# The start of an attention and MLP kernel on one core: summary rows through GpSimd's queue, another order of the first transfers, the third quad's scores ahead of the sums of values

## The chip, the cores and the metric

The kernel runs on one core of a Trainium2 chip. The metric is the device time of one launch in microseconds (us). Before the change the median of three runs is 639.26 us (638.43 to 639.28).

## The reference

Attention over 768 positions in 4 batches and 8 heads of 64 numbers. Each query sees the keys less than 16 positions away and, beside them, 24 summaries of blocks of 32 positions: the maximum of the block's keys and the mean of its values. The result, 3072 tokens of 512 numbers, goes through an MLP.

```
k_sum = k.reshape(B, H, nb, 32, D).max(axis=3)
v_sum = v.reshape(B, H, nb, 32, D).mean(axis=3)
scores_l = where(|i - j| < 16, q @ k.T / 8, -1e9)
scores_s = q @ k_sum.T / 8 + log(32)
a = softmax(concatenate([scores_l, scores_s]))
x = a @ concatenate([v, v_sum])          # -> [3072, 512]
h = x @ w_in                             # [3072, 2048]
out = (h * erf(softplus(h))) @ w_out     # [3072, 512]
```

The inputs q and k are drawn eight times larger than v, and all is f32.

## The kernel before

**Tiles.** The tokens are cut into 6 chunks of 512 tokens. A chunk's attention is done in 4 *quads*, one for each pair of heads (24 quads, numbered from 0; quads 0 to 3 belong to the first chunk and are called the first to the fourth below). A chunk's hidden layer is done in 4 *hidden blocks* of 512 hidden numbers, each in four quarters of 128; the stretch of the kernel for one hidden block is a *period* (24 periods). Products of the MLP take each f32 operand as a high and a low part in a shorter format and add three matmuls (L625, L690); only the output products of the first two periods use f32 as it is (L686).

**One quad.** TensorE makes scores (L501) into one bank or two, for the first quads with the mask added by matmuls (L485, L486). VectorE takes row maxima (L525, later L521), negates and scales them (L540), ScalarE makes eight exponentials with their row sums (L531), VectorE adds 1e-9, inverts (L535, L543) and scales by the sums (L547). TensorE turns the probabilities (L561), ScalarE copies them (L565), TensorE multiplies them by the values (L586), and the result x is split into high and low (L268 and L602).

**One period.** Four hidden products (L625, each of 12 matmuls, one quarter of a hidden block) go into banks h0 and h1 in turn (the first four into h0, h1, o0, o1). From each, ScalarE takes a tanh (L636) and VectorE or ScalarE a copy of h (L268). Then ScalarE takes logarithms (L649) and error functions (L654), VectorE multiplies (L661 in the first two periods, L666 later) and splits (L268, L673), and TensorE adds the output product (L690, L686). ScalarE's tanh, logarithm and erf are in different tables, and a change of table is an instruction of its own (L891).

**Summaries.** For the first batch K's block maxima come from the natural layout of K (tiles `kf`, L424, VectorE). The sums of V come from TensorE: `vsum_first` multiplies six tiles of V by a matrix `pick` (L430, six matmuls into a bank named `vs`), ScalarE copies the result (L433), and rows of it are laid into the tile of values of each of the first four quads: for the first quad by a copy on GpSimd (L436), for the other three by a DMA that SP issues (L438). For later batches K and V are loaded in natural layout into a shared tile `rows` (L372, L373), VectorE reduces them (L380, L381), TensorE turns V's sums (L388), ScalarE copies them (L390). GpSimd lays K's maxima into later quads' K tiles (L456, 28 copies).

**Transfers.** All loads go through SP's queue in one order: K and Q of the first four quads (L413, L414), V for the sums (`vt`, L418), V rows of the first four quads (`vwf`, L421), 16 units of weights (`rw`, L301, 1 MB each; VectorE puts their numbers together in three steps, then ScalarE casts the high part, L268, and VectorE takes the low part), then later quads' K, Q and V (L451, L447, L465, L469). A load that has to wait for a tile to come free, or for data to send, holds up what stands behind it in the queue.

**What sets the order.** Every step is recorded in a `Plan` with the engines that can do it and a cost for each. `Plan.due` gives each step a due time by TensorE's order, and `Plan.order` plays the engines against each other and picks, whenever an engine is free, the step with the lowest key: its number (TensorE) or due time (the others), plus an offset from the table `TUNE` (step number: offset, price of a change of table, choice of table, engine). The instructions are then issued in the order found. TensorE may pull a step forward only near the start (a window of 60 steps for steps under 330). In the last loop, until a bank named o3 is first written, `busy` (L728) puts filler matmuls on zeros where the plan has TensorE waiting over 0.3 us; 18 of them stand ahead of everything.

```
busy(math.ceil((gap + (0.8 if free_at < 16.0 else 0.2)) / 0.11) if gap > 0.3 else 0)
```

Of the kernel before, what the change touches and what calls it, by code (L numbers as in the profile page):

```python
# [26 lines left out]
NB = T // 64  # L27
NI = NB // 2
NT = T // 128
NS = 24  # L30
LW = 96
NK = LW + NS
# [8 lines left out]
NN = 2  # L41
TABLE = 1.29
PEN = 1.5
TUNE = {138: (-4.0, 1.5, 0, None), 161: (13.0, 1.5, 0, None), 168: (0.0, 3.0, 0, None), 198: (0.0, 1.5, 0, 'DVE'), 207: (13.0, 1.5, 0, None), 212: (13.0, 1.5, 0, None), 240: (-9.0, 1.5, 0, None), 241: (-5.0, 1.5, 0, None), 371: (22.0, 1.5, 0, None), 498: (0.0, 1.5, 0, 'ACT'), 511: (3.0, 1.5, 0, None)}
LAT = {"PE": 0.25, "DVE": 0.2, "ACT": 0.24, "POOL": 0.3, "SP": 2.0}


# [130 lines left out]
def block_attention_mlp(ctx: ExitStack, tc: tile.TileContext, q_t, k_nat, k_win, v_tok, v_nat, v_win, w_in, w_out, out):  # L178
    nc = tc.nc
# [7 lines left out]
    def sb(shape, dtype, name, tag=None):  # L187

        n = math.prod(shape[1:])
        if n % 128 == 0:  # L190
            return pool.tile(shape, dtype, name=name, tag=tag or name)
        t = pool.tile([128, -(-n // 128) * 128], dtype, name=name, tag=tag or name)[0:shape[0], 0:n]
        return t if len(shape) == 2 else t.rearrange("p (a b) -> p a b", a=shape[1]) if len(shape) == 3 else t.rearrange("p (a b c) -> p a b c", a=shape[1], b=shape[2])

    def ps(name, tag):
        return psum.tile([128, 2, 512] if tag == "pa" else [128, 512], F32, name=name, tag=tag)
# [50 lines left out]
    vsum = sb([NK, NP, 128], F32, "vsum")  # L247
# [7 lines left out]
    def pe(us, fn, r=(), w=(), **kw):  # L255
        return P.add({"PE": us}, lambda e: fn(), r, w, **kw)

    def on(us, fn, r=(), w=(), **kw):
        return P.add(us, lambda e: fn(engines[e]), r, w, **kw)

    def act(us, fn, r=(), w=(), **kw):
        return P.add({"ACT": us}, lambda e: fn(), r, w, **kw)

    def dma(kb, fn, r=(), w=(), hold=2.0, **kw):
        return P.add({"SP": max(0.45, kb / 350.0)}, lambda e: fn(), r, w, hold=hold, **kw)
# [135 lines left out]
    st = {}  # L401
# [24 lines left out]
    def vsum_first(bank):  # L426
        def go(t):
            if t == 0:
                tiles[bank] = ps("vs", bank)
            nc.tensor.matmul(tiles[bank][0:NK], lhsT=pick[:, 20 - 4 * t:140 - 4 * t], rhs=vts[t // 3][:, t % 3], start=(t == 0), stop=(t == 5))  # L430
        for t in range(6):
            pe(0.87, lambda t=t: go(t), [f"vt{t // 3}"], [bank])
        act(0.5, lambda: nc.scalar.copy(vsum[LW:NK], tiles[bank][LW:NK].rearrange("s (p c) -> s p c", p=NP)), [bank], [f"vsum0{p}" for p in range(NP)])  # L433
        for p in range(NP):
            if p == 0:
                on({"POOL": 1.1}, lambda e: e.tensor_copy(st[0]["vw"][LW:NK], vsum[LW:NK, 0:1, :].to_broadcast([NS, NB, 128])), ["vsum00"], ["vwg0"])  # L436
            else:
                dma(100, lambda p=p: nc.sync.dma_start(out=st[p]["vw"][LW:NK], in_=vsum[LW:NK, p:p + 1, :].to_broadcast([NS, NB, 128])), [f"vsum0{p}"], [f"vwg{p}"])  # L438


    def load_quad(qd):
# [283 lines left out]
    def busy(n):  # L725

        for _ in range(n):
            nc.tensor.matmul(idle[:, 0:256], lhsT=zeros[:, 0:128], rhs=zeros, start=True, stop=True)  # L728
# [10 lines left out]
    for p in range(3):  # L739
        ksum_first(p)  # L740
        scores(p, banks[p])
        softmax(p, banks[p])
    vsum_first("o2")
    ksum_first(3)
    scores(3, banks[3])
# [133 lines left out]
    free = {"PE": 5.0, "DVE": 1.4, "ACT": 4.2, "POOL": 5.2, "SP": 0.7}  # L879
    plan = P.order(free, lambda n: 60 if n < 330 else 0, TUNE, "exp")  # L880
    sets = {"exp": "exp_and_others", "log": "natural_log_exp_and_others", "sig": "sigmoid_and_others"}
    free_at, filling = free["PE"], True
    for o in plan:
        if o["on"] == "PE":
            filling = filling and "o3" not in o["w"]
            if filling:
                gap = o["start"] - free_at
                busy(math.ceil((gap + (0.8 if free_at < 16.0 else 0.2)) / 0.11) if gap > 0.3 else 0)
            free_at = o["end"]
        if "load" in o:  # L890
            nc.scalar.preload_act_table_set(sets[o["load"]])  # L891
        o["fn"](o["on"])
# [40 lines left out]
```

## Time and profile before

| what | before |
|---|---|
| median of three runs | 639.26 us |
| the profiled execution | 639.46 us |
| its span on the core | 637.6 us |
| TensorE busy | 631.5 us (99%) |
| VectorE busy | 393.8 us (62%) |
| ScalarE busy | 432.7 us (68%) |
| GpSimd busy | 18.6 us (3%) |
| granted clock of TensorE | 1.00 |

The lines quoted below come from one profiled execution. In the views of groups and of the timeline a line gives start and length in us, the engine, the source line and operation, the tile written and the tiles read, the count, and in brackets the idle time ahead of it with what ended it. PE is TensorE's matmuls, PEld its weight loads, DVE VectorE, ACT ScalarE, POOL GpSimd, SP the engine that issues transfers. The chain of waits is followed back from the last instruction; its lines give start, length, engine, tile and line.

### The profile page before, as it was taken

To read this page: it belongs to the slowest core of one execution; us is meant where nothing else is said; L and a number is where in the kernel's file an instruction comes from. 1 tells how busy PE (TensorE), PEld (TensorE's weight loads), DVE (VectorE), ACT (ScalarE), POOL (GpSimd) and SP (SyncE) were. 2 spreads that over 40 slices of the span, in tenths; PEclk is the share of its full clock that TensorE was granted. 3 is DMA by queue.
4 is the path that set the end of the run, shared out by engine and by line. 5 is a ranking of instruction groups with operands and counts; after the bars stand their busy time and mean duration, and the time that the engine had idled before them with its cause. 6 is when DMAs were issued, how large, how long until landed. Compare 5 with 4: busy or idle time off the path is not lost.

```text
span 637.6 us, 10591 instructions
## 1 busy us (share of the span) xinstructions
PE 631.5 (99%) x4288; PEld 505.8 (79%) x4288; DVE 393.8 (62%) x507; ACT 432.7 (68%) x779; POOL 18.6 (3%) x56
## 2 busy tenths in 40 slices
PE   9999999999999999999999999999999999999997
PEld 6786566888888888878888888888888888888886
DVE  4999999873975574576655745745555454334432
ACT  5749999969868567676494785675865852863460
POOL 2100011000000000000000000000000000000000
PEclk9999999999999999999999999999999999999999
DMA  8999775753454062752242640223451103140013
GB/s 325 271 343 348 254 227 178 251 180 110 174 161 129 1 213 96 225 182 64 66 149 90 205 149 1 79 73 139 145 177 33 32 1 133 66 133 1 1 62 136
DMA packets 28485, 89.33 MB, mean 140 GB/s; under 512 B 3028, under 2 KB 8468, under 8 KB 23316
## 3 DMA queue, kind: packets, MB, share of 16 engines
q1 hardware_dynamic: 27860, 88.13, 41.9%
q8 instruction: 34, 0.56, 0.4%
q10 hardware_dynamic: 576, 0.52, 0.2%
q14 instruction: 15, 0.12, 0.1%
HBM read 75.89 MB, written 10.49 MB: 135 GB/s over the span
## 4 chain that ended last, share of the span: by engine, by line
PE 91%; ACT 4%; DVE 2%; DMA 2%; issue 0%; SPq 0%; DVEq 0%
PE ops L690 38%; PE h L625 36%; PE px L586 4%; PE pa L501 3%; PE pa L561 3%; PE ops L686 2%; PE idle L728 2%; ACT L891 1%; DMA out<-rows 1%; PE vs L430 1%; DMA rows<-k_nat 1%; ACT wt L649 1%; PE h L501 0%; ACT wt L636 0%; ACT pr L531 0%; DVE hc L268 0%
## 5 line engine op out<-in xcount | busy, mean ns | idle before, releaser
L625 PE MATMUL h<-xh,w 128*128 128x512 f32 x768 | 250.0, 395 | 0.3 <-ACT vsum L390 0.3
L690 PE MATMUL ops<-w,gh 128*128 128x512 f32 x704 | 223.2, 392 | 0.0
L625 PEld LDWEIGHTS h<-xh,w 128*128 128x128 f32 x768 | 144.1, 188 | 32.0 <-issue 1.4
L636 ACT ACTIVATE wt<-h 128x512 f32<-128x512 f32 x96 | 57.3, 598 | 154.1 <-DVE hc L268 84.3
L690 PEld LDWEIGHTS ops<-w,gh 128*128 128x128 f32 x704 | 132.6, 188 | 27.8
L625 PE MATMUL h<-xl,w 128*128 128x512 f32 x384 | 149.4, 389 | 0.0
L891 ACT ACT_TABLE_LOAD x106 | 136.0, 1283 | 1.8
L690 PE MATMUL ops<-w,gl 128*128 128x512 f32 x352 | 137.2, 390 | 0.0
L268 DVE COPY hc<-h 128x512 f32<-128x512 f32 x88 | 60.7, 690 | 123.1 <-PE h L625 115.1
L625 PEld LDWEIGHTS h<-xl,w 128*128 128x128 f32 x384 | 72.2, 188 | 15.2 <-issue 1.0
L690 PEld LDWEIGHTS ops<-w,gl 128*128 128x128 f32 x352 | 66.1, 188 | 13.2
L666 DVE TENSOR_TENSOR hc<-wt,hc 128x1024 f32<-128x1024 f32 x44 | 52.5, 1222 | 19.0 <-ACT wt L654 19.0
L649 ACT ACTIVATE wt<-wt,stats 128x1024 f32<-128x1024 f32 x48 | 55.3, 1153 | 0.6
L531 ACT ACTIVATE pr<-pr,stats 128x120 f32<-128x120 f32 x128 | 48.8, 382 | 9.0 <-DVE stats L540 8.9
L673 DVE TENSOR_TENSOR gl<-hc,gh 128x1024 fp32r<-128x1024 f32 x44 | 52.4, 1220 | 0.2
L654 ACT ACTIVATE wt<-wt 128x1024 f32<-128x1024 f32 x48 | 49.2, 1054 | 0.3
L268 DVE CAST gh<-hc 128x1024 fp32r<-128x1024 f32 x44 | 30.1, 690 | 24.8 <-PE ops L690 24.1
L535 DVE TENSOR_SCALAR stats<-stats 128x8 f32<-128x8 f32 x24 | 4.2, 175 | 43.1 <-ACT pr L531 41.5
L686 PE MATMUL ops<-a32s,gw 128*128 128x512 f32 x64 | 29.0, 594 | 0.0
L565 ACT COPY ptr<-pa 120x1024 f32<-120x1024 f32 x24 | 24.1, 1004 | 3.3 <-PE pa L561 3.3
L456 POOL COPY kw<-ksum 128x96 f32<-128x96 f32 (+1 forms) x28 | 13.1, 480 | 443.5 <-DMA kw<-k_win 383.8
L586 PEld LDWEIGHTS px<-ptr,vw 120*64 120x64 f32 x640 | 20.3, 138 | 5.4 <-issue 3.1
(109 smaller groups left out, 523.1 us busy)
## 6 DMA issues: line engine op xcount, KB each, us to landing
w<-dr SPq DMA_DIRECT2D x20, 1024.0 KB
kw<-k_win SPq DMA_DIRECT2D x20, 480.0 KB
rw<-w_in SPq DMA_DIRECT2D x8, 1024.0 KB
rw<-w_out SPq DMA_DIRECT2D x8, 1024.0 KB
vw<-v_win SPq DMA_DIRECT2D x20, 384.0 KB
qb<-q_t SPq DMA_DIRECT2D x20, 256.0 KB
rows<-v_nat SPq DMA_DIRECT2D x12, 384.0 KB
rows<-k_nat SPq DMA_DIRECT2D x12, 384.0 KB
```

The costliest lines, as they stand in the source:

```text
L268: e.copy(o, i) if e is nc.scalar else e.tensor_copy(o, i)
L531: nc.scalar.activation(s["pr"][:, j], s["pr"][:, j] if qd >= MQ else s["sc"][j // NI][:, i * NK:(i + 1) * NK], AF.Exp, scale=0.125, bias=s ...
L586: nc.tensor.matmul(xo[r, o], lhsT=s["vw"][:, j, r], rhs=s["pt"][:, a, o], start=True, stop=True)
L625: nc.tensor.matmul(hs[k, f][:, 0:T], lhsT=w[m], rhs=xt[ch, cc][x], start=(cc == 0 and n == 0), stop=(cc == 3 and n == 2))
L636: nc.scalar.activation(wt[k, f // 2][:, f % 2], hs[k, f][:, 0:T], AF.Tanh, scale=0.5)
L649: act(1.06, lambda n=n: nc.scalar.activation(wt[k, n], wt[k, n], AF.Ln, scale=-0.49999994, bias=half_b), [s], [s], table=("log",))
L654: act(0.96, lambda n=n: nc.scalar.activation(wt[k, n], wt[k, n], AF.Erf, scale=-1.0), [s], [s], table=("sig",), after=after)
L666: e.tensor_tensor(hc[k, n], wt.pop((k, n)), hc[k, n], op=ALU.mult)
L673: e.tensor_tensor(gs[k, n][1], hc.pop((k, n)), f32(gs[k, n][0]), op=ALU.subtract)
L686: nc.tensor.matmul(os_[ch, t], lhsT=x[0][:, i % 2, t * 128:(t + 1) * 128], rhs=w32["o", g, i // 2][:, i % 2], start=first, stop=last)
L690: nc.tensor.matmul(os_[ch, t], lhsT=x[y][:, i % 2, t * 128:(t + 1) * 128], rhs=w[m], start=first and n == 0, stop=last and n == 2)
L891: nc.scalar.preload_act_table_set(sets[o["load"]])
```

## The change

Three pieces of code change.

1. Rows of V's summaries for the second to fourth quad (L438) are sent by GpSimd's queue instead of SP's.
2. The rule for fillers is the same wherever they stand: the gap plus 0.3 us (it was plus 0.8 before 16 us of the plan and plus 0.2 after).
3. `TUNE` has 117 entries instead of 11. They move steps up to number 797 of the plan, and by that transfers, steps of VectorE and ScalarE and, up to about 260 us, of TensorE; behind that TensorE's order is the same.

```diff
-TUNE = {138: (-4.0, 1.5, 0, None), 161: (13.0, 1.5, 0, None),
...
+TUNE = {0: (-450.0, 1.5, 0, None), 1: (-443.0, 1.5, 0, None), 2: (-339.0, 1.5, 0, None), 3: (-556.0, 1.5, 0, None),
...
             if p == 0:
                 on({"POOL": 1.1}, lambda e: e.tensor_copy(st[0]["vw"][LW:NK], vsum[LW:NK, 0:1, :].to_broadcast([NS, NB, 128])), ["vsum00"], ["vwg0"])
             else:
-                dma(100, lambda p=p: nc.sync.dma_start(out=st[p]["vw"][LW:NK], in_=vsum[LW:NK, p:p + 1, :].to_broadcast([NS, NB, 128])), [f"vsum0{p}"], [f"vwg{p}"])
+                on({"POOL": 2.5}, lambda e, p=p: e.dma_start(out=st[p]["vw"][LW:NK], in_=vsum[LW:NK, p:p + 1, :].to_broadcast([NS, NB, 128])), [f"vsum0{p}"], [f"vwg{p}"])
...
             if filling:
                 gap = o["start"] - free_at
-                busy(math.ceil((gap + (0.8 if free_at < 16.0 else 0.2)) / 0.11) if gap > 0.3 else 0)
+                busy(math.ceil((gap + 0.3) / 0.11) if gap > 0.3 else 0)
```

The entries of `TUNE` say little by themselves, so here is what they do at three places. First the order on TensorE where the third quad's scores (into the banks o0 and o1, here `o_281` and `o_282`) meet the sums of values (`vs`). Before:

```order
L728 MATMUL idle<-zeros 128x256
L430 MATMUL vs<-vt,pick 120x512 x2
L485 LDWEIGHTS small
L485 MATMUL o_281<-mask_h,small 128x480
...
L430 MATMUL vs<-vt,pick 120x512 x4
L561 MATMUL pa<-ident,prf 120x128 x8
L728 LDWEIGHTS zeros
```

Two of the six sums stood ahead of the third quad's scores, behind fillers. The same place on TensorE after the change (the scores' banks are now `o_262` and `o_263`; the first row is the last of the second quad's scores):

```order
L501 MATMUL h_211<-ksum,qf 64x24
L485 LDWEIGHTS small
L485 MATMUL o_262<-mask_h,small 128x480
...
L501 MATMUL o_263<-ksum,qf 64x24
L430 MATMUL vs<-vt,pick 120x512 x6
L561 MATMUL pa<-ident,prf 120x128 x8
L485 LDWEIGHTS small
```

The third quad's scores now follow the second quad's directly, and all six sums come behind them.

The second place is SP's queue of transfers, from the first unit of weights on. Before:

```order
L301 DMA rw<-w_in 128x2048
L414 DMA qf<-q_t 128x512
L421 DMA vwf<-v_win 96x1024 x2
L301 DMA rw<-w_in 128x2048
L438 DMA vwf<-vsum 24x8x128
L421 DMA vwf<-v_win 96x1024
L438 DMA vwf<-vsum 24x8x128
L301 DMA rw<-w_in 128x2048
L421 DMA vwf<-v_win 96x1024
L301 DMA rw<-w_in 128x2048
L438 DMA vwf<-vsum 24x8x128
L373 DMA rows<-v_nat 128x768
```

The three transfers of summary rows stood between V rows and weights. SP's queue after the change:

```order
L301 DMA rw<-w_in 128x2048
L414 DMA qf<-q_t 128x512
L421 DMA vwf<-v_win 96x1024
L301 DMA rw<-w_in 128x2048
L421 DMA vwf<-v_win 96x1024 x2
L301 DMA rw<-w_in 128x2048 x2
L421 DMA vwf<-v_win 96x1024
L373 DMA rows<-v_nat 128x768
L301 DMA rw<-w_out 128x2048
L372 DMA rows<-k_nat 128x768
L451 DMA kw<-k_win 128x960
L373 DMA rows<-v_nat 128x768
```

The summary rows have left it. A second load of `rows<-v_nat` has moved ahead of later weights. They stand on GpSimd now, behind its copy for the first quad:

```order
L251 MEMSET pick 32x1 x4
L436 COPY vwf<-vsum 24x1024
L438 DMA vwf<-vsum 24x8x128 x3
L456 COPY kw<-ksum 128x4x24 x8
L456 COPY kw<-ksum 128x8x24 x8
```

Ahead of the place shown, SP's first transfers are reordered too: before they ran K, Q, K, Q, K, `vt`, Q, `vt`, K, and now Q, K, Q, Q, K, K, K, `vt`, `vt`.

The third place is VectorE near 273 us of the profile of before, where it takes the maxima of a later batch's K (L380). Before:

```order
L268 COPY hc<-h 128x512 x3
L380 TENSOR_REDUCE ksum<-rows 128x24
L268 COPY hc<-h 128x512
L515 TENSOR_TENSOR pr<-pa,mask_sb 128x960
L268 CAST xh<-px 128x512
L521 TENSOR_REDUCE stats<-pr 128x8
```

The maxima stood between the third and the fourth copy of a period. On VectorE after the change, from the last two of these copies on:

```order
L268 COPY hc<-h 128x512 x2
L515 TENSOR_TENSOR pr<-pa,mask_sb 128x960
L268 CAST xh<-px 128x512
L521 TENSOR_REDUCE stats<-pr 128x8
L602 TENSOR_TENSOR xl<-px,xh 128x512
L540 TENSOR_SCALAR stats<-stats 128x8
L381 TENSOR_REDUCE vs_sum<-rows 128x24
L380 TENSOR_REDUCE ksum<-rows 128x24
```

The maxima now come behind the softmax's row maxima and behind the sums of V.

On ScalarE the order of the first periods' functions changes as well: it loads tables 13 times instead of 16 up to the last erf of the third hidden block, and 108 times instead of 106 in all. The scaling by the sums of the fourth quad moves from VectorE to ScalarE (as eight instructions), one cast of x moves from ScalarE to VectorE, and two copies of h in this stretch move from VectorE to ScalarE.

More of the change, by code (lines that the diff above doesn't have):

```diff
@@ L43 @@
 PEN = 1.5
-TUNE = {138: (-4.0, 1.5, 0, None), 161: (13.0, 1.5, 0, None), 168: (0.0, 3.0, 0, None), 198: (0.0, 1.5, 0, 'DVE'), 207: (13.0, 1.5, 0, None), 212: (13.0, 1.5, 0, None), 240: (-9.0, 1.5, 0, None), 241: (-5.0, 1.5, 0, None), 371: (22.0, 1.5, 0, None), 498: (0.0, 1.5, 0, 'ACT'), 511: (3.0, 1.5, 0, None)}
+TUNE = {0: (-450.0, 1.5, 0, None), 1: (-443.0, 1.5, 0, None), 2: (-339.0, 1.5, 0, None), 3: (-556.0, 1.5, 0, None), 4: (-259.0, 1.5, 0, None), 5: (-402.0, 1.5, 0, None), 6: (-246.0, 1.5, 0, None), 7: (-93.0, 1.5, 0, None), 8: (-221.0, 1.5, 0, None), 9: (-144.0, 1.5, 0, None), 10: (-86.0, 1.5, 0, None), 13: (50.0, 1.5, 0, None), 14: (-105.0, 1.5, 0, None), 15: (-87.0, 1.5, 0, None), 68: (-196.0, 1.5, 0, None), 70: (-296.0, 1.5, 0, None), 75: (301.0, 1.5, 0, None), 79: (118.0, 1.5, 0, 'DVE'), 91: (-176.0, 1.5, 0, None), 94: (-157.0, 1.5, 0, None), 107: (92.0, 1.5, 0, None), 108: (39.0, 1.5, 0, None), 109: (39.0, 1.5, 0, None), 110: (175.0, 1.5, 0, None), 115: (103.0, 1.5, 0, None), 124: (92.0, 1.5, 0, None), 127: (168.0, 1.5, 0, None), 128: (139.0, 1.5, 0, None), 130: (546.0, 1.5, 0, None), 131: (177.0, 1.5, 0, None), 132: (332.0, 1.5, 0, None), 138: (333.0, 1.5, 0, None), 140: (65.0, 1.5, 0, 'DVE'), 152: (-172.0, 1.5, 0, None), 154: (485.0, 1.5, 0, None), 155: (511.0, 1.5, 0, None), 157: (147.0, 1.5, 0, None), 169: (265.0, 1.5, 0, 'DVE'), 176: (-138.0, 1.5, 0, None), 178: (-89.0, 1.5, 0, None), 180: (171.0, 1.5, 0, None), 181: (123.0, 1.5, 0, None), 184: (233.0, 1.5, 0, None), 191: (4.0, 8.0, 1, None), 195: (43.0, 1.5, 0, None), 201: (347.0, 1.5, 0, None), 202: (-53.0, 2.0, 0, None), 206: (228.0, 1.5, 0, None), 209: (133.0, 1.5, 0, None), 210: (765.0, 1.5, 0, None), 211: (348.0, 1.5, 0, None), 227: (387.0, 1.5, 0, None), 230: (194.0, 1.5, 0, None), 240: (-501.0, 1.5, 0, None), 243: (279.0, 1.5, 0, None), 244: (426.0, 1.5, 0, None), 247: (-372.0, 1.5, 0, None), 253: (289.0, 1.5, 0, None), 255: (177.0, 1.5, 0, None), 267: (-182.0, 1.5, 0, 'ACT'), 275: (-378.0, 1.5, 0, None), 276: (142.0, 1.5, 0, None), 279: (-120.0, 1.5, 0, None), 281: (285.0, 1.5, 0, None), 303: (314.0, 1.5, 0, None), 305: (-218.0, 1.5, 0, 'ACT'), 311: (-231.0, 1.5, 0, 'ACT'), 316: (231.0, 1.5, 0, None), 320: (96.0, 3.0, 1, None), 325: (172.0, 1.5, 0, None), 327: (-158.0, 1.5, 0, None), 335: (223.0, 1.5, 0, None), 336: (311.0, 1.5, 0, None), 338: (-72.0, 1.5, 0, None), 341: (185.0, 1.5, 0, None), 342: (266.0, 1.5, 0, None), 343: (913.0, 1.5, 0, None), 345: (469.0, 1.5, 0, None), 346: (435.0, 1.5, 0, None), 366: (-404.0, 1.5, 0, None), 383: (-204.0, 1.5, 0, 'ACT'), 446: (231.0, 1.5, 0, None), 472: (-514.0, 1.5, 0, None), 480: (315.0, 1.5, 0, None), 481: (189.0, 2.0, 1, None), 489: (-218.0, 1.5, 0, None), 509: (171.0, 1.5, 0, None), 519: (-96.0, 1.5, 0, None), 529: (112.0, 1.5, 0, None), 531: (98.0, 1.5, 0, None), 545: (169.0, 1.5, 0, None), 552: (90.0, 1.5, 0, None), 553: (251.0, 1.5, 0, None), 567: (132.0, 1.5, 0, None), 591: (176.0, 1.5, 0, None), 593: (194.0, 1.5, 0, None), 594: (232.0, 1.5, 0, None), 599: (236.0, 1.5, 0, None), 603: (444.0, 1.5, 0, None), 621: (319.0, 1.5, 0, None), 624: (291.0, 1.5, 0, None), 638: (198.0, 1.5, 0, None), 675: (190.0, 1.5, 0, None), 680: (189.0, 1.5, 0, None), 682: (215.0, 1.5, 0, None), 692: (-123.0, 1.5, 0, None), 700: (184.0, 1.5, 0, None), 705: (-398.0, 1.5, 0, None), 717: (163.0, 1.5, 0, None), 721: (-149.0, 1.5, 0, None), 722: (244.0, 1.5, 0, None), 732: (103.0, 1.5, 0, None), 733: (34.0, 1.5, 0, None), 740: (123.0, 1.5, 0, None), 754: (259.0, 1.5, 0, None), 789: (-79.0, 7.0, 0, None), 797: (-110.0, 1.5, 0, None)}
```

## The prediction

> **What bounds the kernel now.** I read the page first, then the chain that ended last, TensorE's timeline and waits, the stages, and then the start engine by engine.
>
> ```profile
> span 637.6 us, 10591 instructions
> PE 631.5 (99%) x4288; PEld 505.8 (79%) x4288; DVE 393.8 (62%) x507; ACT 432.7 (68%) x779; POOL 18.6 (3%) x56
> ```
>
> TensorE is busy 99% of the span, so only less work of its own, or less waiting, can shorten the run. Its work is the same in both programs except for filler matmuls (L728), which compute nothing and stand where it would have to wait. The chain shows them:
>
> ```profile
> 1.06 4.02 PE idle L728 x18
> 6.05 1.90 PE pa L501 x37
> ...
> 10.09 2.29 PE idle L728 x20
> ...
> 20.62 0.66 PE idle L728 x6
> ...
> 25.41 2.18 PE idle L728 x19
> 27.59 0.87 PE pa L561 x8
> 28.47 1.08 PE px L586 x32
> 29.55 2.97 PE h L625 x12
> ...
> 39.50 1.08 PE px L586 x32
> ...
> 41.48 1.87 PE idle L728 x17
> ```
>
> A last group stands in TensorE's timeline, just ahead of the first output product (L686):
>
> ```profile
> 53.21 1.05 PE L728 MATMUL idle<-zeros 128*128 128x256 bf16 x8
> 54.09 5.32 PE L686 MATMUL ops<-a32s,gw 128*128 128x512 f32 x12
> ```
>
> From there to the end no filler is left. What TensorE waits for is short:
>
> ```profile
> PE vt L388 <- ACT wt L636: 0.8, 1, 0.8
> PE px L586 <- ACT wt L636: 0.3, 1, 0.3
> PE h L625 <- ACT vsum L390: 0.3, 1, 0.3
> ```
>
> The stages show where other engines come close to being the bound (columns: length; PE, PEld, DVE, ACT, POOL busy; clock, DMA share, GB/s):
>
> ```profile
> 4.00:14.00 10.00, 10.00 (x175) 7.32 (x173) 6.21 (x12) 4.21 (x24) 0.94 (x9) 1.00 1.02 374
> 30.00:50.00 20.00, 20.00 (x177) 16.00 (x180) 18.59 (x23) 11.08 (x15) 1.46 (x2) 1.00 0.99 345
> 50.00:110.00 60.00, 59.71 (x344) 37.16 (x335) 58.76 (x72) 58.64 (x106) 4.65 (x6) 1.00 0.71 244
> 110.00:150.00 40.00, 40.00 (x299) 32.81 (x298) 28.55 (x39) 33.17 (x60) 1.60 (x3) 1.00 0.58 197
> ```
>
> From 50 to 110 us VectorE and ScalarE are full too (98%). Then they have a sixth to a quarter of their time free.
>
> **Term 1, the fillers: -3.1 us.** The new program holds 60 fillers, not 88; 18 at the front are in both. So 70 become 42: 14 ahead of the second quad's scores, 20 ahead of the third quad's transposes, 8 ahead of the last quarter of the first hidden block. One takes 0.11 us (2.29/20, 2.18/19, 1.87/17 in the chain), and 28 x 0.11 = 3.1 us. The work ahead of the first output product is the same in both orders, so it would start at 54.1 - 3.1 = 51.0 us. That holds only if no wait takes a filler's place, so I follow the inputs.
>
> ```profile
> 4.02 0.95 DVE L424 TENSOR_REDUCE ksum<-kf 128x24 f32<-128x768 f32 x1 [2.87 <-DMA kf<-k_nat]
> 6.46 0.95 DVE L424 TENSOR_REDUCE ksum<-kf 128x24 f32<-128x768 f32 x1 [1.49 <-DMA kf<-k_nat]
> 7.99 1.22 DVE L525 TENSOR_REDUCE stats<-pa 128x4 f32<-128x480 f32 x2 [0.57 <-PE pa L501]
> 10.24 0.36 ACT L531 ACTIVATE prf<-pa,stats 128x120 f32<-128x120 f32 x1 [5.79 <-DVE stats L540]
> 18.46 0.36 ACT L531 ACTIVATE prf<-o,stats 128x120 f32<-128x120 f32 x1 [2.62 <-DVE stats L540]
> 21.94 1.01 ACT L565 COPY ptr<-pa 120x1024 f32<-120x1024 f32 x1
> ```
>
> - *First transfers.* The queue is full, so what goes ahead delays what follows, at 374 GB/s. One Q (0.26 MB, 0.7 us) now goes ahead of the first K: its maxima end at 4.02 + 0.7 + 0.95 = 5.7 us, still before the scores' start at 6.05. No cost. Two Q more (0.52 MB, 1.4 us) go ahead of the second K: it is there at 7.9 instead of 6.46, its maxima at 8.8. The 14 fillers from 7.9 to 9.4 us cover that. The first quad's row maxima (1.22) queue behind it, then the third K's (0.95), and ScalarE's first exponentials start near 11.0, not 10.24.
> - *Third quad.* ScalarE waited 2.62 us for the third quad's scores, behind sums of values on TensorE. Now they follow the second quad's at once, end near 13.7, and ScalarE runs through. A block of exponentials takes 2.75 us (half of 10.24 to 18.46 less that wait): 11.0 + 3 x 2.75 = 19.2 us, where it was 21.2. The copy of the first turned probabilities then ends 2.0 us before its 22.95, and TensorE comes for it 1.5 us earlier. Covered.
> - *Summaries of V.* GpSimd now issues three rows of summaries, behind its copy for quad 0:
>
> ```profile
> 10.11 0.35 SPq L301 DMA_DIRECT2D rw<-w_in x1
> 21.94 0.97 SPq L438 DMA_DIRECT2D vwf<-vsum x1
> 43.96 0.33 SPq L373 DMA_DIRECT2D rows<-v_nat  x1
> 21.98 1.77 POOL L436 COPY vwf<-vsum 24x1024 f32<-24x1024 f32 x1 [16.35 <-ACT vsum L433]
> 108.56 2.34 POOL L456 COPY kw<-ksum 128x96 f32<-128x96 f32 x1 [0.19 <-DVE ksum L380]
> 269.30 3.76 DMA rows<-k_nat
> ```
>
> SP's queue stood still from 10.5 to 21.9 us, since the next in it waited for these sums; every later load stood behind. Freed, they follow without a gap. One thing is worse: the second quad's V rows now stand ahead of three weight units and wait until VectorE has read the first V rows. It did so just before 43.96 us. Now that stands ahead of three operations (about 3.1 us by rows of their kind), with VectorE 1.5 us early, so at 39.4. The V rows and the first unit (1.4 MB at 345 GB/s, 4.2 us, and 2.5 us to land) are there at 46; VectorE wants the unit near 48. No cost; if they went out as late as before it would be 50.7, and 2 us at most.
>
> GpSimd's issue of a transfer is in no row of this trace. Bounds for its time T: below, SP's 0.97 us for the same rows; above, GpSimd's longest instruction, 2.34 us. I take 2.0, nearer to GpSimd's own rows. Landing: a K row took 3.76 us, 1.05 of it for its 0.39 MB, so 2.5 us or so behind the issue. The copy ends at 19.9 + 1.8 = 21.7 us, so quad k's rows are there at 24.2 + kT. The values products of quads 1 and 3 stood at 28.47 and 39.50; with leads of 1.5 and 3.1 us they come at 27.0 and 36.4. At T = 2.0 the rows are there at 26.2 and 30.2. No cost up to T = 2.8.
>
> The Trainium skill speaks against this step ("SBUF — State Buffer", SBUF: two separate sides): a DMA from GpSimd's queue has its descriptors written by GpSimd, which VectorE's two-port copies lock out, with 0.62 us alone and 3.1 us beside such a copy. By 3.1 us as T the sum would be 0.3 us worse; no run here shows it yet.
>
> - *The first output product* waits for the first gated block, by this piece of the chain:
>
> ```profile
> 46.14 0.94 ACT w L268
> ...
> 52.42 1.23 DVE gw L661
> ```
>
> Its multiplication ended at 53.65, 10.3 us after the last quarter of the block began (43.35). That quarter now begins 20 fillers, 2.2 us, earlier, at 41.1; on ScalarE a weight's cast (0.94) and a hidden copy leave the piece and a tanh of the copy's length comes in, 0.9 us less: 50.5. Covered, by 0.5 us.
>
> **Term 2, waits that go: -1.1 us.** This is the place of the 0.8 us:
>
> ```profile
> 273.16 0.95 DVE L380 TENSOR_REDUCE ksum<-rows 128x24 f32<-128x768 f32 x1 [2.57 <-DMA rows<-k_nat]
> ```
>
> VectorE sat 2.57 us on a maximum whose K had not landed; a hidden copy, ScalarE's tanh of the same bank and TensorE's transpose (L388) stood behind. Now that maximum comes after the copies and the row maxima of the softmax. The wait goes; next late is the K row itself, for which there are 5 us more. The 0.3 us of L625 stands behind a copy of summaries on ScalarE near 77 us, whose neighbours changed: gone. The 0.3 us of L586, at 523 us, stays: from 260 us on TensorE's order is unchanged.
>
> **Term 3, detours: +0.3 us.** Scores and values products that stood side by side are parted in four cases. 12 matmuls right after a values product took 2.97 us (at 29.55); at the full rate they would take half of this row, 2.72:
>
> ```profile
> 160.65 5.44 PE h L625 x24
> ```
>
> That is 0.25 us each, 1.0 at most; with fewer switches to fillers I take 0.3.
>
> **Term 4, new waits in the full stretch: +0.6 us.** A lead of 3 us at 51 us lasts to 110 us only if VectorE and ScalarE lead as well. Up to the third hidden block's last erf ScalarE loads tables 13 times, not 16:
>
> ```profile
> L891 ACT ACT_TABLE_LOAD x106 | 136.0, 1283 | 1.8
> ```
>
> That is 3 x 1.28 = 3.8 us less. It takes over the fourth quad's scaling by the sums (8 instructions, about 2.4 us) in the stretch where it works 11.08 of 20 us: hidden. VectorE loses that scaling and two hidden copies and gets one cast, by rows of their kind (1.16, 0.69, 0.68) 1.9 us less, and starts its conversions 1.5 us earlier. So both should come out ahead by about as much as TensorE does, with nothing to spare at 98%. I allow 0.6 us; bounds 0 and 3.1, the whole lead. After 110 us five loads come back, 6.4 us, into time that ScalarE has free.
>
> **Sum.** -3.1 - 1.1 + 0.3 + 0.6 = -3.3 us. The profiled execution took 639.46 us, of which 1.9 lie around its span; it would take 636.2. The median of the runs is 0.2 below it, so the forecast is 636.0 us. A difference under 0.2% (1.3 us) can't be told from none.
>
> **Rivals.**
> 1. *VectorE or ScalarE becomes the bound in the full stretch* and takes the lead back: term 4 is 3.1, the rest stays, 638.5 us; half of it, 637.0. For: 58.76 of 60 us busy. Against: both have less to do there. Chance 0.14.
> 2. *Slower: GpSimd issues late.* Quad 3's rows come last, at 24.2 + 3T, wanted at 36.4: its product waits 3T - 12.2. From T = 5.2 on that is more than the 3.3 us won; at T = 6.2 it is 6.4 us, and the run takes 642. For: GpSimd's copies stretch up to 2.34 us beside VectorE, and its transfers now run beside a full queue of SP's. Against: 2.34 is under half of 5.2. Chance 0.08.
> 3. *The change doesn't win what it drops*: the fillers stood for waits that stay, term 1 is nothing and term 4 too, 638.5 us, or 639.3 with the wait of term 2 kept. For: each group stood where an input was due. Against: the third quad's inputs do come 2.0 us earlier. Chance 0.08.
>
> **Numbers.** The forecast has 0.70; its own range goes from 634.8 (no new waits, no detours, the last 0.3 us gone: -4.5) to 637.4 (2 us of new waits). With the first and third rival the range is 634.6 to 638.8. Faster by over 0.2% (below 638.0): the forecast and most of the first rival, 0.80. Within: 0.12. Slower: 0.08.
>
> **What would show it.** Right: the first output product at 51 us after 42 fillers; ScalarE's third exponentials without a wait; GpSimd's three issues under 2.8 us each and no values product (L586) waiting for them; L388 not waiting near 270 us. Term 4 is what TensorE waits between 51 and 110 us. Wrong: waits of several us there, or L586 waiting for GpSimd.

## The result

The changed kernel takes 642.23 us (median of 6 runs, 641.10 to 643.56), the kernel before 638.82 us (6 runs, 638.43 to 639.28). The ratio is 1.0052, 95% interval 1.0037 to 1.0066: slower by half a per cent, where 636.0 us had been forecast, with 638.8 us as the upper end. One execution of a kernel further down (the first of the last group) took 1052.69 us at a granted clock of 0.56; its median is that of the other ten.

The page of the changed kernel:

```profile
span 640.8 us, 10532 instructions
PE 632.2 (99%) x4260; PEld 503.8 (79%) x4260; DVE 395.0 (62%) x505; ACT 437.9 (68%) x790; POOL 23.5 (4%) x59
```

28 fillers are gone, and TensorE is as busy as before: something else took their place. Of the waits of TensorE that the prediction named, the 0.8 us of L388 and the 0.3 us of L625 are gone too; three others stand there now:

```profile
PE px L586 <- issue: 1.6, 1, 1.6
...
PE h L625 <- DVE hc L268: 0.6, 1, 0.6
PE px L586 <- DVE stats L535: 0.6, 1, 0.6
```

To see where the time went, the start of the same instruction is read in both traces. At a place with the same work behind it in both, the difference is the lead of the changed kernel (us, negative where it is behind):

| instruction of TensorE | before | after | lead |
|---|---|---|---|
| fourth quad's scores | 21.11 | 19.59 | +1.5 |
| third quad's transposes | 27.43 | 29.48 | -2.1 |
| second quad's values product | 28.40 | 31.09 | -2.7 |
| first output product (L686) | 54.09 | 54.71 | -0.6 |
| an output product near 120 us | 120.73 | 121.70 | -1.0 |
| a hidden product, order the same from here | 260.62 | 264.39 | -3.8 |
| the transpose that had waited 0.8 us (L388) | 275.40 | 278.44 | -3.0 |

So there are two losses: 4.2 us between the fourth quad's scores and the second quad's values product (some of it made good by the fillers that are gone behind it), and 2.8 us between 120 and 260 us. The gain at 273 us came, 0.7 us.

This is the chain of waits in the first of them, in the changed kernel (start, length, what):

```profile
21.79 0.45 PE px L586 x8
22.24 1.61 issue
23.85 0.92 PE px L586 x24
24.77 1.62 PE pa L561 x8
26.39 3.25 PE idle L728 x20
29.64 0.87 PE pa L561 x8
30.52 0.57 issue
31.09 1.15 PE px L586 x32
```

Three things are seen. TensorE stops for 1.6 us in the middle of the first quad's values product, where nothing of the program releases it. Then 8 transposes take 1.62 us, not 0.87, and 20 fillers 3.25 us, not 2.2. At last the second quad's product waits 0.57 us. The stages around it show why the transposes and fillers are slow (length; PE, PEld, DVE, ACT, POOL busy; granted clock, the busy share of the core's DMA engines, GB/s):

```profile
21.70:25.10 3.40, 1.79 (x41) 1.49 (x36) 3.40 (x6) 1.32 (x2) 1.96 (x4) 0.99 1.05 260
25.10:28.40 3.30, 3.30 (x18) 2.57 (x17) 3.30 (x6) 2.22 (x8) 0.00 (x0) 0.50 1.03 257
```

With TensorE busy 1.79 of 3.40 us, the granted clock was halved for the 3.4 us that followed. Two of the six runs had a mean clock under 1 (642.57 and 643.56 us); the other four took 641.10 to 642.37 us, so the halved clock is not the main loss. GpSimd's timeline shows its three issues:

```profile
21.68 1.98 POOL L438 DMA_DIRECT2D vwf<-vsum  x3
```

and its row in the view of transfers has their median time from issue to landing at the end:

```profile
vwf<-vsum POOLq DMA_DIRECT2D x3, 96.0 KB, 10.0
```

GpSimd issues its three transfers in 0.76, 0.61 and 0.61 us, but they land (their last data and the signal that tells of it are there) 9.3, 10.0 and 11.4 us after their issue. The first, for the second quad, lands at 31.0 us: that is what its values product waits for at 30.52 (the view names another releaser, L535, which was done at 30.45). Its first packet moves at 27.0 us, 5.3 us after the issue. By the forecast it would have been there at 26.2.

### The profile page after: what moved, and what is told of

It is laid out like the page before. It is cut to its first block, busy times and chain, and to the rows that moved or that the text cites. A ratio compares the mean times of both kernels' runs of the same rounds, so it can differ in the third digit from the quotient of the medians.

```text
span 640.8 us, 10532 instructions
## 1 busy us (share of the span) xinstructions
PE 632.2 (99%) x4260; PEld 503.8 (79%) x4260; DVE 395.0 (62%) x505; ACT 437.9 (68%) x790; POOL 23.5 (4%) x59
## 4 chain that ended last, share of the span: by engine, by line
PE 93%; ACT 5%; issue 1%; DVE 1%; ACTq 0%
PE h L625 38%; PE ops L690 37%; PE px L586 4%; PE pa L561 3%; PE pa L501 3%; PE ops L686 2%; ACT L891 2%; PE idle L728 1%; ACT wt L636 1%; PE vs L430 1%; DVE hc L268 1%; ACT wt L649 1%; PE h L501 0%; ACT wt L654 0%; ACT pr L531 0%
## 5 line engine op out<-in xcount | busy, mean ns | idle before, releaser
L625 PE MATMUL h<-xh,w 128*128 128x512 f32 x768 | 252.7, 397 | 0.8 <-DVE hc L268 0.6
L690 PE MATMUL ops<-w,gh 128*128 128x512 f32 x704 | 226.2, 393 | 0.0
L625 PEld LDWEIGHTS h<-xh,w 128*128 128x128 f32 x768 | 144.1, 188 | 34.8 <-DVE hc L268 2.4
L625 PE MATMUL h<-xl,w 128*128 128x512 f32 x384 | 149.6, 390 | 0.0
L268 DVE COPY hc<-h 128x512 f32<-128x512 f32 x83 | 57.4, 691 | 119.5 <-PE h L625 105.5
L625 PEld LDWEIGHTS h<-xl,w 128*128 128x128 f32 x384 | 72.2, 188 | 15.1 <-issue 1.0
L456 POOL COPY kw<-ksum 128x96 f32<-128x96 f32 (+1 forms) x28 | 16.6, 605 | 441.7 <-DMA kw<-k_win 371.3
L686 PE MATMUL ops<-a32s,gw 128*128 128x512 f32 x64 | 29.8, 597 | 0.0
L535 DVE TENSOR_SCALAR stats<-stats 128x8 f32<-128x8 f32 x24 | 4.9, 205 | 36.6 <-ACT pr L531 35.4
```

The lines of the kernel that those rows point to most:

```text
L268: e.copy(o, i) if e is nc.scalar else e.tensor_copy(o, i)
L625: nc.tensor.matmul(hs[k, f][:, 0:T], lhsT=w[m], rhs=xt[ch, cc][x], start=(cc == 0 and n == 0), stop=(cc == 3 and n == 2))
L686: nc.tensor.matmul(os_[ch, t], lhsT=x[0][:, i % 2, t * 128:(t + 1) * 128], rhs=w32["o", g, i // 2][:, i % 2], start=first, stop=last)
L690: nc.tensor.matmul(os_[ch, t], lhsT=x[y][:, i % 2, t * 128:(t + 1) * 128], rhs=w[m], start=first and n == 0, stop=last and n == 2)
```

## The experiments

**What delays the rows.** Three theories: "queue" (a transfer issued beside a full queue of SP's waits behind what is queued), "GpSimd" (its way of sending is slow) and "program" (TensorE's stop at 22 us is the loss). First, SP issues the rows again, at the place where GpSimd's would stand, all else as in the changed kernel:

```diff
-on({"POOL": 2.5}, lambda e, p=p: e.dma_start(out=st[p]["vw"][LW:NK], ...
+on({"POOL": 2.5}, lambda e, p=p: nc.sync.dma_start(out=st[p]["vw"][LW:NK], ...
```

> The changed kernel with the three transfers of summary rows issued by SP again; every engine's order of work is otherwise the changed kernel's, and SP's queue stands still again until the sums are there. Theory 'queue' (a transfer issued beside a full queue of SP's waits behind what is queued): the rows for the second quad are there by 25 us, its values product comes near 28.5 us instead of 31.1, and 640.0 us. Theory 'GpSimd' (GpSimd's own way of sending is slow, whatever is queued): the same, 640.0. Theory 'program' (the lost time is TensorE's 1.8 us without instructions at 22 us and the half clock after it, and the rows are only in time by accident): the stall and 642 us stay unless the freed queue also brings the program earlier.

Measured: 639.84 us (ratio 1.0012, 1.0002 to 1.0021), 2.4 us less than the changed kernel. Its chain:

```profile
22.50 0.82 issue
23.32 0.92 PE px L586 x24
24.24 1.02 PE pa L561 x8
25.26 2.18 PE idle L728 x20
27.45 0.87 PE pa L561 x8
28.32 1.08 PE px L586 x32
```

The second quad's product comes at 28.3 us, the stop is half as long and the clock stays. Its first output product starts at 51.95 us; 51.0 had been forecast. So the new way of sending the rows costs 2.8 us up to this place (54.71 against 51.95), most of the 3.7 us that were missing there. This doesn't tell "queue" from "GpSimd"; the next one does. ScalarE issues them (`nc.scalar.dma_start`), and SP's queue stays full:

> The changed kernel with the three transfers of summary rows issued by ScalarE's queue; SP's queue stays full. Theory 'queue': the rows land 8 to 9 us after their issue near 21.5, so near 30 us, and the time stays at 641.5 to 642.5. Theory 'GpSimd': they land 2.5 to 4 us after their issue, by 25.5 us, the second quad's values product comes near 29 us, and 640 us or less. Theory 'program': 642, with the stall at 22 us as before.

Measured: 647.92 us (1.0133, 1.0118 to 1.0148). TensorE's timeline shows the second quad's product waiting:

```profile
33.63 1.98 PE L586 MATMUL px<-ptr,vwf 120*64 120x64 f32 x32 [3.22 <-issue]
```

and the stage around it, in the columns used above, its clock:

```profile
33.20:39.90 6.70, 6.27 (x42) 5.30 (x43) 3.60 (x6) 4.21 (x10) 0.00 (x0) 0.50 0.95 315
```

Issued at 21.79 us, the first transfer moved its first packet at 27.36 and its last of data at 32.1, 10.3 us after the issue, though GpSimd had nothing to do with it. The last signal of its landing came at 33.53, and the product started at 33.63. "GpSimd" falls as the reason for so long a way. Half clock for 6.8 us followed the wait. Then this part of the change alone, in the kernel before (`nc.gpsimd.dma_start`, all orders as before):

> The kernel before with this part of the change alone: the three transfers of summary rows issued by GpSimd, all orders else those of before. Theories 'queue' and 'GpSimd': the rows land near 31 us instead of before 28.4, the second quad's values product waits 2 to 3 us for them, and the run takes 641 to 641.5 us. Theory 'program': a stall of TensorE without a releaser appears in the second quad's stretch only if the fetch of its program is late there; else 639 us.

Measured: 644.74 us (1.0082, 1.0067 to 1.0097). The rows land 8.8 us after their issue, at 32.2 us; TensorE's timeline shows the product behind them:

```profile
32.29 1.15 PE L586 MATMUL px<-ptr,vwf 120*64 120x64 f32 x32 [4.12 <-issue]
```

With the wait, and 3.4 us of halved clock behind it, the kernel takes 5.9 us more, over twice what was expected. The last run of this group keeps GpSimd and empties the queue: a tiny transfer on SP waits for the second quad's rows.

```diff
+def rows(e, p=p):
+    e.dma_start(out=st[p]["vw"][LW:NK], ...
+    if p == 2:
+        nc.sync.dma_start(out=dram.tile([1, 128], F32, name="held", tag="held"), in_=st[1]["vw"][LW:LW + 1, 0])
...
```

> The changed kernel (rows by GpSimd) with one tiny extra transfer in SP's queue, behind the second quad's V rows, that must wait until the second quad's summary rows have landed; so nothing more is queued on SP while GpSimd's rows travel. It computes the same. Theory 'queue': the rows for the second quad land within 4 us of GpSimd's issue (by 26 us, against 9.3 us and 31.0 us in the changed kernel). Rival 'GpSimd': they land 8 to 10 us after their issue as before. The time says little, since all later loads go out later: 639.5 to 643 us.

Measured: 640.44 us (1.0030, 1.0019 to 1.0041). The view of transfers:

```profile
vwf<-vsum POOLq DMA_DIRECT2D x3, 96.0 KB, 4.0
```

and the stage in which the rows travel:

```profile
21.70:25.10 3.40, 1.94 (x39) 1.73 (x38) 3.40 (x7) 1.63 (x2) 1.58 (x3) 1.00 0.66 136
```

The median time to landing is 4.0 us, where it was 10.0; the first row was issued at 21.30, moved at 22.64 and landed at 25.81. VectorE is as busy as before (3.40 of 3.40 us); the DMA share fell from 1.05 to 0.66. "Queue" holds. Even with every later load sent out at 26 us instead of 13, the run is 1.8 us faster than the changed kernel.

**What stops TensorE at 22 us.** The profile has transfers of instructions, in pieces of 16 KB; that those meant here are TensorE's is inferred. In the changed kernel one moved from 21.29 to 22.57 us, and TensorE, which had run through the small matmuls of the fourth quad's scores, stood from 22.24 to 23.85. In the three kernels above that keep the changed order, it stopped at the same place too (0.82 us with rows on SP, 1.37 us with rows by ScalarE, 1.46 us with SP held), and each stop ended 1.3 to 1.4 us after the end of such a piece. If it ran out of program, more instructions ahead at the same time should move that:

```diff
-busy(WARM)
+for _ in range(36):
+    nc.tensor.matmul(idle[:, 0:128], lhsT=zeros[:, 0:128], rhs=zeros[:, 0:128], start=True, stop=True)
```

> The changed kernel with its 18 warm-up fillers of 256 columns replaced by 36 of 128 columns: the same time at the front, 36 instructions more on TensorE. Theory 'program' (TensorE stalls at 22 us since the next piece of its program arrives late): the piece is asked for 36 instructions of work earlier, in the slow sums of values; the stall of 1.8 us at 22 us goes or moves to another place, and the clock is not halved at 25 us. Rivals 'queue' and 'GpSimd' (the first quad's values product itself waits for something of GpSimd's): the stall stays where it is. By all three the second quad's product still waits for rows at 31 us, so the time stays within 641.0 to 642.5 us.

Measured: 642.18 us (1.0047, 1.0029 to 1.0066). TensorE's timeline:

```profile
21.73 1.15 PE L586 MATMUL px<-ptr,vwf 120*64 120x64 f32 x32
...
29.66 1.15 PE L586 MATMUL px<-ptr,vwf 120*64 120x64 f32 x32 [2.70 <-DVE stats L535]
```

The piece of program now came at 16.39 us, the first quad's product runs through, and the clock stays at 1.00. And the time is the same: the second quad's product still waits, now 2.70 us, for rows that land at 29.6. (The two traced executions span 639.4 and 640.8 us, but only the changed kernel's had the halved clock; its executions at full clock span 639.3 to 640.6 us.) The stop was real and hid behind the rows. So the instructions ahead of the piece decide when it comes. It doesn't take a full queue to be late: with rows on SP the DMA share was 0.49 while the piece moved, and TensorE still stopped for 0.82 us. Whether the full queue made the other stops longer isn't shown.

**What costs 2.8 us in the middle.** Both plans are made in one kernel, and the list that is issued takes one up to a given step, then the other (fillers by a table, the summary rows sent by SP throughout):

```diff
-plan = P.order(free, lambda n: 60 if n < 330 else 0, TUNE, "exp")
...
+plans = {"after": ordered(TUNE, "POOL"), "before": ordered(TUNE_BEFORE, "SP")}
...
+for which, upto in PIECES:
+    end = next((o["start"] for o in plans[which] if o["n"] == upto), 1e9)
+    for o in plans[which]:
+        if o["n"] not in done and o["start"] < end:
...
```

> The changed kernel's orders up to the first output product (with the summary rows issued by SP), then the orders of the kernel before until TensorE's order is the same in both (near 260 us), then the changed ones. Theory 'middle' (the changed order between 54 and 260 us costs 3.1 us by itself, whatever the start is): the lead of 2.1 us at the first output product stays, 0.75 us come on top at 273 us, and the run takes 636.0 us. Rival 'start' (the changed start leaves VectorE and ScalarE with more to do, and so any middle loses the lead): 638.5 to 639 us.

> The start of the kernel before, fillers included, up to its first output product, then the changed kernel's orders to the end. Theory 'middle': 3.1 us lost between 54 and 260 us, 0.75 us won at 273 us: 641.2 us. Rival 'start': the middle costs little behind the old start: 638.0 to 639 us.

> The kernel before with the changed orders from 260 us on alone, by which VectorE takes the maxima near 273 us behind the softmax's. Theory (term 2 of the prediction): TensorE's wait of 0.8 us there goes and nothing takes its place, 638.1 us. Rival: the wait moves to another place and the time stays at 638.8 us.

Measured: 638.03 us (0.9980, 0.9968 to 0.9992), 642.14 us (1.0054, 1.0040 to 1.0069) and 638.42 us (0.9993, 0.9985 to 1.0001). The lead of each over the kernel before, at the places of the first table:

| kernel | 54 us | 120 us | 260 us | 275 us |
|---|---|---|---|---|
| changed | -0.6 | -1.0 | -3.8 | -3.0 |
| rows on SP | +2.2 | +1.8 | -1.0 | -0.2 |
| old start, changed middle | -2.0 | -2.7 | -5.6 | -4.8 |
| changed start, old middle | +1.6 | +0.1 | +0.2 | +1.0 |
| old, changed tail | -0.2 | -0.2 | -0.2 | +0.7 |

Wherever the changed order runs from 120 to 260 us it loses 2.8 to 2.9 us, from a lead of +1.8 or of -2.7; the old order there loses nothing. So the middle costs by itself. (The start of the one with the old start and the changed middle was not quite the old one: its loads moved, and two values products waited 1.2 and 0.7 us. Its traced execution, 644.26 us, is also 2.1 us above its median.) A lead at the start is known to 0.8 us only: in three kernels with the same start (the one before, that with the changed tail, and the last of the next group) the first output product came at 54.09, 54.26 and 53.49 us. The changed start with the old middle missed its 636.0 by 2.0 us: 1.4 us of its lead went between 57 and 65 us, at this wait in TensorE's timeline:

```profile
64.58 0.33 PE L388 MATMUL vt<-ident,vs_sum 128*120 128x128 f32 x1 [1.19 <-ACT wt L636]
```

There the old order lets a transpose wait for a bank behind a VectorE that has no gap (the prediction's first rival, in the old order); the changed order doesn't lose there. The tail alone gave 0.8 us in the trace; by the runs it can't be told from none.

In the changed middle no scores stand beside a values product any more; in the old one six pairs do between 120 and 260 us, and three more before 120 us, which the changed order parts too. Ten pairs of the kernel before were parted from 275 us on, first by four hidden products:

> The kernel before, in which from 275 us on the scores of ten quads stand four hidden products (2.7 us) earlier on TensorE, so that they no longer stand side by side with a values product; the order of every other engine is the same. Theory (a parted pair costs what the traces show where hidden or output products follow a product of small matmuls, 0.2 to 0.25 us, and there are eight such in the changed middle, not four): 2.0 to 2.5 us more, 640.7 to 641.2 us. Rival (a parted pair is nearly free, as the prediction took it at 0.3 us for four): 639.5 us.

> As the run before, but the ten scores stand only two hidden products (1.36 us) earlier: the copy of the turned probabilities that frees their bank ends 1.5 us ahead of them in the kernel before, so no wait comes with the move. Theory: a parted pair costs 0.2 to 0.3 us by itself, 640.6 to 641.6 us. Rival (nearly free): 639.2 us or less. If the first were right, the six pairs parted between 120 and 260 us in the changed kernel make up 1.2 to 1.8 of the 2.8 us lost there.

> The same ten scores two hidden products earlier, in a program in which nothing else is issued in another order and all other waits stand where they stood (in the last two kernels the rebuilt order also put waits elsewhere before 271 us). Theory: 0.23 us for each parted pair, as the last five periods of the run before showed, and 0.4 us more in the five periods with a transpose of sums behind the values product: 2.3 to 4.3 us more than the kernel before, 641.0 to 643.0 us. Rival (nearly free): 639.2 us or less.

Measured: 660.64 us (1.0341, 1.0327 to 1.0354), 648.46 us (1.0150, 1.0133 to 1.0167), 642.36 us (1.0054, 1.0040 to 1.0068). The first two are misses for the question: in the first, each scores waited 1.2 us for its bank, and in both the rebuilt list had waits standing elsewhere, with 5.2 us lost from 120 to 260 us, where TensorE's order is the same (why was not followed). In the third only the ten pairs differ. Its time has 3.3 us for them, and its waits show that part of this is another thing:

```profile
PE vt L388 <- ACT wt L636: 1.7, 5, 0.3
```

In the first five periods a transpose of sums (L388) stands behind the values product and now waits 0.33 us. The last five have none. Two values products among these last, three periods apart, in the kernel before and in that one:

```profile
424.42 1.15 PE L586 MATMUL px<-ptr,vw 120*64 120x64 f32 x32
...
499.34 1.15 PE L586 MATMUL px<-ptr,vw 120*64 120x64 f32 x32
```

```profile
426.75 1.15 PE L586 MATMUL px<-ptr,vw 120*64 120x64 f32 x32
...
502.37 1.15 PE L586 MATMUL px<-ptr,vw 120*64 120x64 f32 x32
```

74.92 us against 75.62: 0.70 in three periods, 0.23 us for a parted pair. Ten of these and the five waits, less the 0.8 us that L388 had waited at the first of these places before, make 3.2 us, about what was measured. By this estimate six of them are 1.4 of the 2.8 us. Three hidden products in the changed middle (near 171, 201 and 221 us) start 0.2 us late, and the matmul behind each comes 0.1 us late as well: 0.9 us together. What holds them was not followed, and the last 0.5 us stay open.

**Together.** The changed order up to 120 us with rows on SP, the old one to 260 us, the changed tail; then with 36 short warm-up fillers; then also with 8 fillers instead of 20 ahead of the third quad's transposes.

> The changed kernel's orders up to 120 us (summary rows issued by SP), then the orders of the kernel before until 260 us, then the changed ones. Theory: the changed start and the changed full stretch keep 1.8 us of lead at 120 us (that is what the kernel with rows on SP had there), the old order from 120 to 260 us costs nothing, and 0.7 us come at 273 us: 636.2 us. Rival 'full stretch' (VectorE or ScalarE are behind in any case and the lead goes after 120 us too): 638 to 639 us.

> The same with 36 warm-up fillers of 128 columns instead of 18 of 256, so that TensorE's program is fetched 36 instructions of work earlier. Theory 'program': the stall of 0.8 us in the first quad's values product goes and, as the rows are no longer late, shows in the time now: 635.4 us. Rival (another input is late by then): 636.2 us, the same as without.

> The last one with 8 fillers instead of 20 ahead of the third quad's transposes. If the fillers stand for no wait there: 1.3 us less, 634.1 us. If they stand for one (the copy of the second quad's turned probabilities, which in the kernel with rows on SP ended 1.0 us ahead of the third quad's transposes, or the V rows): 634.6 to 635.4 us, with a wait in their place.

Measured: 637.50 us (0.9977, 0.9968 to 0.9986; no trace of it is read), 637.90 us (0.9993, 0.9980 to 1.0007) and 637.40 us (0.9978, 0.9969 to 0.9988). The first and third are faster than the kernel before by 0.2%, but they fall 1.3 us and at least 2.0 us short of what was expected. In the second's trace the stop is gone and the lead is 2.3 us at 120 and 2.4 us at 275 us (span 635.1), but its runs spread up to 641 us, so that a gain over the first, or over the kernel before, isn't shown. In the third, waits took the fillers' place, as in TensorE's timeline:

```profile
26.40 1.06 PE L561 MATMUL pa<-ident,prf 128*120 128x128 f32 x8 [0.68 <-ACT prf L531]
```

## Why the prediction was wrong

- **Term 1, the fillers.** The count and the price (at full clock) held: 28 fewer. The step that failed is "Landing: a K row took 3.76 us ... so 2.5 us or so behind the issue". That row is of 269 us, where the DMA share was 0.60. At 21 us the change itself fills the queue ("Freed, they follow without a gap" stands one paragraph earlier), the share was 1.05, and the landing took 9.3 us. The product was wanted at 27.0 us and the rows were forecast for 26.2; they came at 31.0. The issue, which the prediction weighed, was the harmless part: 0.61 to 0.76 us, not 2.0.
- **The second rival** had the right side at 0.08, and among its reasons the right cause ("its transfers now run beside a full queue of SP's"), but it priced a slow issue, T, and looked at the fourth quad's rows; the second quad's came too late first. That its 642 us, for a T of 6.2, is what was measured is luck: T was 0.6 to 0.8.
- **The rule of the Trainium skill** ("SBUF — State Buffer", SBUF: two separate sides) that GpSimd's transfers suffer beside VectorE's copies was not put to the test: while the three issues ran (21.68 to 23.66 us) VectorE was busy, but with an operation on two tiles (L324), a reciprocal (L543) and row maxima (L525), not with a copy. It isn't needed either: each issue took 0.61 to 0.76 us, and with ScalarE issuing beside the full queue the way was as long. Another page of the Trainium skill fits: by "DMA: Bandwidth & Descriptors" (Issuing engines are not separate DMA queues) transfers of all issuing engines share the same 16 DMA engines. That page's rule of turns between queues (Queues, rings and completion order), one whole packet of descriptors from each, gives a turn in descriptors and not as a time; beside the full queue the first packet came 4.9 to 5.6 us after the issue here, and 1.3 us with the queue held.
- **TensorE's program** was no step at all, so its cost was put at nothing. Before, transposes and fillers stood where the piece came (19.39 to 20.62 us); that they covered it is argued, not shown by a run.
- **The first transfers** and the third quad's scores went as said: the first maxima ended at 5.6 us (5.7 forecast), ScalarE ran from the second into the third exponentials without a wait, and the turned probabilities' copy ended 1.5 us earlier (2.0 forecast).
- **Term 2.** Right: the wait of 0.8 us went, and 0.7 to 0.8 us came. The 0.3 us near 77 us went as well, in a stretch that lost time on the whole.
- **Term 3** was mis-sized: nine pairs were parted, not four (three before 120 us and six behind), and by the estimate of 0.23 us each that is 2.1 us, not 0.3. The row with 0.25 us was on the table; discounting it for "fewer switches to fillers" had no row behind it.
- **Term 4.** 0.6 us was allowed. Between 54 and 120 us the changed kernel lost 0.4 us on the whole, and it waited 0.6 us at one hidden product. Its chain from 45.85 us to this place is ScalarE's without a gap, which started late since the first hidden block came late:

```profile
71.86 0.49 ACT wt L636
...
72.37 0.70 DVE hc L268
```

TensorE resumed at 73.12 us. The late starts between 120 and 260 us, where engines seemed to have room, weren't foreseen.
- **The range** "634.6 to 638.8" leaves out the 639.3 us that the prediction's own third rival gives. The measured time lies beyond both.

## What to carry to other kernels

A queue that stands still is also an empty one: whoever frees it must price every small transfer that is wanted soon beside the data that now follows without a gap, and the nearest row is one from a stretch with the same DMA share. Send such a small transfer before the flood of loads is let go, or let the flood wait for it. A filler may cover more than the wait that the plan saw, so look for what else is fetched there before taking it away.

## What the hardware showed that was not expected

- A transfer of 96 KB issued by GpSimd took 3.7 to 4.5 us from issue to landing at a DMA share of 0.66 and 8.8 to 11.4 us at 1.02 to 1.05. One issued by ScalarE at 1.02 had its last data there after 10.3 us.
- Instructions come by DMA in pieces of 16 KB (about 1.2 us each). In four kernels TensorE stopped for 0.8 to 1.6 us until 1.3 to 1.4 us after the end of such a piece; 36 more instructions ahead, in the same time, brought the piece 4.9 us earlier, and the stop went.
- The granted clock fell to 0.50 for 3.4 us after a stretch of 3.4 us with TensorE busy for 1.79. By the Trainium skill ("TensorE: Matmul & The Clock Gate", What's actually happening) it falls after an idle window of about that length; here half of one was enough once, while 1.94 of 3.40 us in the run with SP held was not followed by it.
- VectorE's L535 on 8 numbers a partition took 1.01 us instead of 0.17 while GpSimd's copy (L436) ran, and ended with it:

```profile
20.46 1.27 POOL L436 COPY vwf<-vsum 24x1024 f32<-24x1024 f32 x1 [14.86 <-ACT vsum L433]
...
20.75 1.01 DVE L535 TENSOR_SCALAR stats<-stats 128x8 f32<-128x8 f32 x1
```
